# All first folds on VectorE, output additions in 128 pieces of 2 KB, a planner that counts transfers, and new ranks

## The chip, the cores and the metric

The kernel runs on one core of one Trainium2 chip. The metric is the device time of one execution in microseconds (us). In the texts, TensorE (PE in the profile) does matrix multiplications, VectorE (DVE) and ScalarE (ACT) work on elements, GpSimd (POOL) only issues DMA transfers here, and SyncE (SP) issues the other DMA transfers. What can be told from no change in a measurement of this kernel is about 0.5%, which is 1.9 us.

## What is computed

The output is a gated sum of two branches over the same x of 2048 x 512 numbers (float32). Branch a is a two-dimensional Fourier transform, a product with a filter, and the transform back. Branch b is a two-layer network with 1792 hidden columns.

```python
def _A_ref(x, w_r, w_i):
    B, S, D = x.shape
    X = jnp.fft.rfft2(x, axes=(-2, -1))
    X = X * (w_r + 1j * w_i)
    return jnp.fft.irfft2(X, s=(S, D), axes=(-2, -1))

def _B_ref(x, w1, b1, w2, b2):
    h = _gelu(jnp.einsum("bsd,df->bsf", x, w1) + b1)
    return jnp.einsum("bsf,fd->bsd", h, w2) + b2

x = A_x
g = _sigmoid((x * gate_w).sum(-1, keepdims=True))
return g * _A_ref(x, A_w_r, A_w_i) + (1 - g) * _B_ref(x, B_w1, B_b1, B_w2, B_b2)
```

## The kernel before

**Planning.** The program first builds a graph of 1877 steps: `v` for VectorE, `a` for ScalarE, `m` for a group of matmuls, `dma` for a transfer from SyncE, and `dma_pool` and `acc` for transfers from GpSimd. An `acc` adds to what stands at its destination. Each step carries an estimated cost, and a rank from the tuple `RANKS`, one entry for each step in the order in which the graph is built. The entry divided by 100 is the rank. `Graph.schedule` then plays the steps through: an engine that is free takes the ready step of the lowest rank for which buffer slots are free. The order that comes out is the order in which the instructions are written to each engine's queue, and on the chip each queue runs in that order. The ranks have the size of microseconds, but they fix an order and nothing else.

**Forward transform** (`forward(j)`, lines 670 to 767). It is done for 16 row tiles j, in the order `NORD` = 0, 4, 8, 12, 1, 5, 9, 13, 2, 6, 10, 14, 3, 7, 11, 15. Each tile of x (128 x 4 x 128) is folded twice: sums and differences of its halves give `eo`, and sums and differences of the halves of `eo` give `cl`. The second fold is always done on VectorE (line 698). The first fold has two forms. For the first `FOLD_DMA` = 12 tiles it is two VectorE instructions of 128 x 256 (line 684). For the last four, j = 3, 7, 11, 15, x is loaded into `eo`, ScalarE negates half of it (line 678), and GpSimd loads x again in the other order and adds it there. The result is split into a high and a low part (`eoh`, `eol`), and TensorE multiplies them with a table (`pd`), then with another (`py`); the sums are left in `Y[j]`.

**Middle.** `stage1`, `filt` and `stage4` are the short transform over the 16 tiles and the filter, all on VectorE. Beside them TensorE works on the network: `mlp(half, c)` takes half of the hidden columns for a quarter c of the rows. Groups `ph` are the first layer, twelve matmuls each, `po` the second. The result of the first half goes to DRAM (`bacc`); that of the second half is added there by `acc`, except for c = 2.

**Back transform and output.** `inverse(c, h)` runs for four c and two h. It scales the tile (`sw`, `pq`), splits it (`vh`, `vl`), multiplies (`pz`), splits again (`zh`, `zl`) and multiplies (`pa`). ScalarE copies half of `pa` to `od` (line 995), two VectorE instructions give `uv` (line 998), and the two output parts are the sum and the difference of the two halves of `uv`. For c = 3 and 0 (`ADD_DMA`) these are formed in DRAM: SyncE stores one half of `uv` to both parts, ScalarE makes the negative of the other half, and GpSimd adds it and its negative. For c = 1 (`SUM_FIRST`) VectorE forms both (`y`, line 1009) and GpSimd adds them to the output, where SyncE has already stored the network's share. For c = 2 VectorE forms both, GpSimd adds the network's first half to them (`y<-bb`), and `last` takes the second half off (`o`, line 1137). `combine(c, h)` reads `bacc` back into `ba` through GpSimd (line 513), multiplies it with 1 − g on VectorE (line 1028) and adds or stores it to the output.

**Queues.** All GpSimd transfers are issued strictly one behind the other, and so are SyncE's. A part of the output, `part(c, h, k)`, is 128 x 2 x 256 numbers, 2 KB in a row for each of 128 rows. In `uv` before, the halves are stored as `uv[:, i]`, and the transfer takes `uv[:, :, 0]` or `uv[:, :, 1]`: two runs of 1 KB that do not touch, so 256 pieces for a transfer of 256 KB. The same holds for `y`, which has rows of 257 numbers of which 256 are taken.

Of the kernel before, what the change touches and what calls it, by code (L numbers as in the profile page):

```python
# [117 lines left out]
FOLD_DMA = 12  # L118
# [51 lines left out]
class Graph:  # L170
# [283 lines left out]
def tile_kernel(ctx: ExitStack, tc: tile.TileContext, xt, w1, w2, b1, b2, x0g, wf, wrev, out, consts):  # L454
# [40 lines left out]
    def v(emit, n, reads, writes, rank=BULK, more=0.0):  # L495
        return add("vec", c_vec(n) + more, 0.12, emit, reads, writes, rank)
# [8 lines left out]
    def dma(emit, kb, reads, writes, rank=FEED, first=None):  # L505
        if first is not None:
            return add("sp", kb / 390, first, emit, reads, writes, rank)
# [747 lines left out]
```

## Time and profile before

| what | value |
|---|---|
| median of 3 runs | 389.84 us (389.78 to 391.7) |
| the profiled execution, its own time | 392.12 us |
| its span, first to last instruction | 390.4 us |
| TensorE busy | 370.8 us, 95% |
| VectorE busy | 325.9 us, 84% |
| ScalarE busy | 229.7 us, 59% |
| GpSimd busy | 64.5 us, 17% |
| granted TensorE clock, mean | 0.975 |
| DMA packets, MB | 53044, 64.30 |

The durations come from the one profiled execution, whose own time is 2.3 us above the median. [...] Where several matmuls follow without a wait, TensorE counts as busy also when the clock granted to it is low, so the clock has to be read beside the busy time. Idle time of an engine on which nothing waits costs nothing.

### The profile page before, as it was taken

The numbers are of one execution on the slowest core, as the hardware profiler recorded it, in microseconds if no ns is written. First come the engines' busy times: TensorE is split into PE (matmuls) and PEld (weight loads), VectorE is DVE, ScalarE is ACT, GpSimd is POOL, SyncE is SP. The second block draws the span as 40 slices with busy tenths as digits, with TensorE's granted clock in tenths as the row PEclk, the third lists the DMA queues.
The fourth block names the chain that finished last, engine by engine and source line by source line (L and its number), as shares of the span: only waits on it lengthen the run. The fifth ranks groups of instructions, "written<-read, shape, count | busy, mean of one in ns | idle before, by whom it ended". The sixth has DMA issues, their size and how long they took to land.

```text
span 390.4 us, 5587 instructions
## 1 busy us (share of the span) xinstructions
PE 370.8 (95%) x1838; PEld 313.5 (80%) x1838; DVE 325.9 (84%) x687; ACT 229.7 (59%) x457; POOL 64.5 (17%) x74
## 2 busy tenths in 40 slices
PE   8999999998999999999999999999978999999980
PEld 6888888886888888888888888888857888788870
DVE  4999998887899699999979998767737767999950
ACT  5865758886757542663665129946925496369400
POOL 0000000220000000121211120023342223423131
PEclk9999999998999999999999999999996999999995
DMA  8955996467772233696795751287688887855276
GB/s 270 372 158 155 311 346 220 97 149 177 222 220 89 61 107 110 111 266 164 138 266 140 225 82 41 71 250 137 98 145 168 186 241 98 133 121 148 82 126 90
DMA packets 53044, 64.30 MB, mean 165 GB/s; under 512 B 4784, under 2 KB 35824, under 8 KB 52240
## 3 DMA queue, kind: packets, MB, share of 16 engines
q1 hardware_dynamic: 41512, 46.39, 36.9%
q0 software_dynamic: 11360, 17.31, 29.0%
q10 hardware_dynamic: 144, 0.26, 0.3%
q8 instruction: 14, 0.23, 0.2%
q14 instruction: 14, 0.11, 0.1%
HBM read 39.69 MB, written 23.21 MB: 161 GB/s over the span
## 4 chain that ended last, share of the span: by engine, by line
PE 70%; DMA 8%; issue 8%; DVE 7%; POOL 3%; ACT 3%; POOLq 0%; SPq 0%; DVEq 0%; ACTq 0%
PE ph L526 31%; PE po L526 30%; PE pz L526 3%; PE pd L526 2%; PE py L526 2%; POOL out L517 2%; DMA eo<-in_xt 2%; DMA ba<-bacc 2%; PE pa L526 2%; DMA out<-uv 1%; DVE uv L998 1%; DMA xr<-in_xt 1%; DMA tf<-tf 1%; ACT ph L1086 1%; DVE y L763 0%
## 5 line engine op out<-in xcount | busy, mean ns | idle before, releaser
L1086 ACT ACTIVATE ph<-ph,b1t 128x512 f32<-128x512 f32 x56 | 36.8, 657 | 47.2 <-PE ph L526 47.0
L945 ACT ACTIVATE sw<-y,al 64x512 f32<-64x512 f32 x32 | 22.9, 721 | 3.6 <-DVE y L808 2.7
L904 DVE TENSOR_TENSOR m<-y,wf 128x514 f32<-128x514 f32 x32 | 20.7, 689 | 0.1
L1122 ACT ACTIVATE o<-po,b2t 128x512 f32<-128x512 f32 x16 | 11.0, 687 | 15.8 <-PE po L526 15.7
L517 POOL DMA_DIRECT2D eo<-in_xt x4 | 5.0, 1256 | 82.1 <-DMA tf<-tf 67.6
L517 POOL DMA_DIRECT2D bacc<-o x12 | 11.2, 983 | 38.7 <-ACT o L1125 35.8
L952 DVE SCALAR_TENSOR_TENSOR pq<-y,al,sw 128x256 f32<-128x256 f32 x32 | 14.5, 480 | 3.4 <-ACT sw L948 3.3
L1125 ACT ACTIVATE o<-po 128x512 f32<-128x512 f32 x12 | 7.0, 594 | 17.1 <-PE po L526 10.2
L1028 DVE SCALAR_TENSOR_TENSOR ba<-gb,ba 128x512 f32<-128x512 f32 x12 | 8.2, 686 | 7.9 <-DMA ba<-bacc 7.9
L526 PE MATMUL pd<-cf,eoh 128*128 128x260 f32 x64 | 13.0, 286 | 1.7 <-DVE x3l L735 1.7
L998 DVE TENSOR_TENSOR uv<-pa,od 128x512 f32<-128x512 f32 x16 | 10.5, 686 | 4.6 <-ACT od L995 4.6
L513 POOL DMA_DIRECT2D ba<-bacc x12 | 10.0, 835 | 24.7 <-DMA bacc<-o 10.0
L517 POOL DMA_DIRECT2D out<-y x8 | 9.0, 1128 | 27.9 <-DVE y L1009 11.0
L526 PEld LDWEIGHTS pd<-cf,eoh 128*128 128x128 f32 x64 | 10.7, 189 | 3.1 <-issue 1.9
L517 POOL DMA_DIRECT2D wa7l<-in_w x1 | 0.9, 924 | 67.4 <-PE po L526 67.4
L760 ACT ACTIVATE y<-pys 64x257 f32<-64x257 f32 x24 | 10.0, 418 | 3.2 <-DVE pys L757 2.8
L995 ACT ACTIVATE od<-pa 128x512 f32<-128x512 f32 x8 | 4.8, 597 | 10.6 <-PE pa L526 10.4
L526 PE MATMUL pd<-cf,eol 128*128 128x130 f32 x64 | 10.5, 254 | 0.0
L948 ACT ACTIVATE sw<-y 1x512 f32<-1x512 f32 x16 | 9.9, 627 | 0.4
L526 PEld LDWEIGHTS pd<-cf,eol 128*128 128x128 f32 x64 | 9.8, 189 | 0.4 <-DVE eol L701 0.2
L517 POOL DMA_DIRECT2D out<-ba x8 | 7.7, 1000 | 12.1 <-DVE ba L1028 7.2
L517 POOL DMA_DIRECT2D y<-bb x8 | 7.6, 954 | 11.0 <-DVE y L1009 6.2
(711 smaller groups left out, 1390.5 us busy)
## 6 DMA issues: line engine op xcount, KB each, us to landing
wf<-in_wf SPq DMA_DIRECT2D x16, 257.0 KB, 3.5
bacc<-o SPq DMA_DIRECT2D x16, 256.0 KB, 4.3
war<-in_w SPq DMA_DIRECT2D x14, 256.0 KB, 2.9
wbr<-in_w SPq DMA_DIRECT2D x14, 256.0 KB, 2.8
xm<-in_xt SPq DMA_DIRECT2D x12, 256.0 KB, 4.5
bacc<-o POOLq DMA_DIRECT2D x12, 256.0 KB, 4.8
ba<-bacc POOLq DMA_DIRECT2D x12, 256.0 KB, 3.5
xr<-in_xt SPq DMA_DIRECT2D x11, 256.0 KB, 4.2
```

Of the source, the lines that this page charges most:

```text
L513: return add("pool", kb / 300, 3.2, lambda: nc.gpsimd.dma_start(dst(), src()), reads, writes, rank)
L517: return add("pool", kb / 150, 3.4, lambda: nc.gpsimd.dma_start(dst(), src(), accum_op=ALU.add), reads, writes, rank)
L526: pe.matmul(ps, w, x, start=start, stop=stop)
L760: a(lambda o=o, i=i: act.activation(Y[j].ap()[o:o + HP, 1], pys.ap()[i:i + HP, 1], AF.Copy), 257, [(pys, 1)], [(Y[j], 1 + k)], 0, more=0.1)
L904: v(lambda mk=mk, k=k, y=y, w=w: vec.tensor_tensor(mk.ap(), y.ap(), w.ap()[:, k:k + 1, :ND].to_broadcast([P, 2, ND]), op=ALU.mult), 514, [ ...
L945: a(lambda sw=sw, y=y, o=o, i=i: act.activation(sw.ap()[o:o + HP], y.ap()[i:i + HP, ::-1, :HD], AF.Copy, scale=al.ap()[i:i + HP, 0:1]), 51 ...
L948: a(lambda sw=sw, y=y, j=j: act.activation(sw.ap()[HP:HP + 1], y.ap()[HP:HP + 1, ::-1, :HD], AF.Copy, scale=math.cos(math.pi * j / NJ)), 5 ...
L952: v(lambda sw=sw, pq_=pq_, y=y, j=j, k=k, op=op: vec.scalar_tensor_tensor(pq_.ap()[:, k], y.ap()[:, k, :HD], al.ap()[:, 1 + j:2 + j], sw.a ...
L998: v(lambda i=i, op=op: vec.tensor_tensor(uv.ap()[:, i], ps.ap()[:, 0], od.ap(), op=op), 512, [ps, od], [(uv, i)], 2)
L1028: vec.scalar_tensor_tensor(b.ap(), gg, 1.0, b.ap(), op0=ALU.subtract, op1=ALU.mult)
L1086: a(lambda f=f, ps=ps: act.activation(ps.ap(), ps.ap(), AF.Gelu_apprx_tanh, bias=b1t.ap()[:, f:f + 1]), 600, [b1t], [ps], 0.9 if half else ...
L1122: a(lambda o=o, ps=ps, q=q: act.activation(o.ap(), ps.ap(), AF.Identity, scale=-1.0, bias=b2t.ap()[:, q:q + 1]), 600, [b2t, ps], [o])
```

## The change

It has four parts.

First, `FOLD_DMA` goes from 12 to 16, the number of tiles. The branch with the negation and the accumulating load is then never taken, and the tiles 3, 7, 11 and 15 are folded like the others: one load and two VectorE instructions. The number of steps stays at 1877.

Second, `uv` is written so that each half of the later sum is contiguous (`uv[:, :, i]` is written, `uv[:, 0]` and `uv[:, 1]` are read), and the sums and negatives are written to a contiguous stretch of their tile (`flat`), except for c = 2. Every transfer from `uv` or from such a stretch then has 128 pieces of 2 KB.

Third, each transfer step takes a token in the planner: `ring` with three slots for GpSimd's, `hw` with eight for SyncE's. A token holds its slot from the start of the step to its estimated end, so no more than so many transfers are out at once in the plan. The tokens become no instruction and no memory. The sizes of two pools and of the scratch memory get names and keep their values.

Fourth, all 1877 ranks are new.

```diff
-FOLD_DMA = 12
+FOLD_DMA = 16
+RING, TI, TTAB = 3, 3, 3
+SCRATCH = 1024
...
 RANKS = (
...
 )
...
-    slots = {..., "ttab": 3, ..., "pm": 4, "ti": 3}
+    slots = {..., "ttab": TTAB, ..., "pm": 4, "ti": TI, "ring": RING, "hw": 8}
...
     def dma(emit, kb, reads, writes, rank=FEED, first=None):
+        reads = [*reads, buf("hw", [1], cls=len(g.steps))]
...
     def dma_pool(dst, src, kb, reads, writes, rank=FEED):
+        reads = [*reads, buf("ring", [1], cls=len(g.steps))]
...
     def acc(dst, src, kb, reads, writes, rank=FEED):
+        reads = [*reads, buf("ring", [1], cls=len(g.steps))]
...
-            v(lambda i=i, op=op: vec.tensor_tensor(uv.ap()[:, i], ps.ap()[:, 0], od.ap(), op=op), 512, [ps, od], [(uv, i)], 2)
+            v(lambda i=i, op=op: vec.tensor_tensor(uv.ap()[:, :, i], ps.ap()[:, 0], od.ap(), op=op), 512, [ps, od], [(uv, i)], 2)
+
+        def flat(y):
+            return y.ap().rearrange("p a b -> p (a b)")[:, :4 * P].rearrange("p (a b) -> p a b", a=2)
+
         if c in ADD_DMA:
             n = Y[c + 8 * h]
-            a(lambda: act.activation(n.ap()[:, :, :2 * P], uv.ap()[:, :, 1], AF.Copy, scale=-1.0), 512, [uv], [n], 2)
+            a(lambda: act.activation(flat(n), uv.ap()[:, 1], AF.Copy, scale=-1.0), 512, [uv], [n], 2)
             for k in range(2):
-                dma(lambda k=k: sp.dma_start(part(c, h, k), uv.ap()[:, :, 0]), 256, [uv], [(OUT[c], 2 * h + k)], 4)
-            acc(lambda: part(c, h, 0), lambda: uv.ap()[:, :, 1], 256, [uv], [(OUT[c], 2 * h)], 4)
-            acc(lambda: part(c, h, 1), lambda: n.ap()[:, :, :2 * P], 256, [n], [(OUT[c], 2 * h + 1)], 4)
+                dma(lambda k=k: sp.dma_start(part(c, h, k), uv.ap()[:, 0]), 256, [uv], [(OUT[c], 2 * h + k)], 4)
+            acc(lambda: part(c, h, 0), lambda: uv.ap()[:, 1], 256, [uv], [(OUT[c], 2 * h)], 4)
+            acc(lambda: part(c, h, 1), lambda: flat(n), 256, [n], [(OUT[c], 2 * h + 1)], 4)
             return
...
-            v(lambda w=w, op=op: vec.tensor_tensor(w.ap()[:, :, :2 * P], uv.ap()[:, :, 0], uv.ap()[:, :, 1], op=op), 512, [uv], [w])
+            v(lambda w=w, op=op: vec.tensor_tensor(w.ap()[:, :, :2 * P] if c == 2 else flat(w), uv.ap()[:, 0], uv.ap()[:, 1], op=op), 512, [uv], [w])
             if c in SUM_FIRST:
-                acc(lambda k=k: part(c, h, k), lambda w=w: w.ap()[:, :, :2 * P], 256, [w], [(OUT[c], 2 * h + k)], 4)
+                acc(lambda k=k: part(c, h, k), lambda w=w: flat(w), 256, [w], [(OUT[c], 2 * h + k)], 4)
...
-    nc = bacc.Bacc("TRN2", ..., dynamic_dma_scratch_size=1024)
+    nc = bacc.Bacc("TRN2", ..., dynamic_dma_scratch_size=SCRATCH)
```

Some ranks of steps that the next section names, before and after: the addition of `uv30` to the output 266.11 and 259.21, that of `ba030` to the same place 262.02 and 265.58; the last group of `pa11` 359.59 and 362.46; the first and the last of the final 14 matmul groups 371.75 and 376.56 before, 363.31 and 368.08 after; the last two additions of y, 369.51 and 370.46 before, 368.13 and 369.66 after.

More of the change, by code (lines that the diff above doesn't have):

```diff
@@ L465, in tile_kernel @@
     vec, act, pe, sp = nc.vector, nc.scalar, nc.tensor, nc.sync
-    slots = {"xr": 3, "xm": 4, "wra": 3, "wrb": 2, "t2k": 7, "e2": 4, "z": 4, "ttab": 3, "xhl": 2, "wa": 2 * FA, "wb": 2 * FA, "hid": 2 * FA,
-             "so": 2, "ba": 2,  "pf": 2, "pm": 4, "ti": 3}
+    slots = {"xr": 3, "xm": 4, "wra": 3, "wrb": 2, "t2k": 7, "e2": 4, "z": 4, "ttab": TTAB, "xhl": 2, "wa": 2 * FA, "wb": 2 * FA, "hid": 2 * FA,
+             "so": 2, "ba": 2,  "pf": 2, "pm": 4, "ti": TI, "ring": RING, "hw": 8}
     whole = ("xr", "xm", "wra", "wrb", "e2", "z", "ttab", "xhl", "wa", "wb", "hid", "so", "ba", "ctab", "gb")
@@ L1008, in inverse @@
             w = Y[c + 8 * h + 4 * k]
-            v(lambda w=w, op=op: vec.tensor_tensor(w.ap()[:, :, :2 * P], uv.ap()[:, :, 0], uv.ap()[:, :, 1], op=op), 512, [uv], [w])
+            v(lambda w=w, op=op: vec.tensor_tensor(w.ap()[:, :, :2 * P] if c == 2 else flat(w), uv.ap()[:, 0], uv.ap()[:, 1], op=op), 512, [uv], [w])
             if c in SUM_FIRST:
-                acc(lambda k=k: part(c, h, k), lambda w=w: w.ap()[:, :, :2 * P], 256, [w], [(OUT[c], 2 * h + k)], 4)
+                acc(lambda k=k: part(c, h, k), lambda w=w: flat(w), 256, [w], [(OUT[c], 2 * h + k)], 4)
             elif c != 2:
-                dma(lambda w=w, k=k: sp.dma_start(part(c, h, k), w.ap()[:, :, :2 * P]), 256, [w], [(OUT[c], 2 * h + k)], 4)
+                dma(lambda w=w, k=k: sp.dma_start(part(c, h, k), flat(w)), 256, [w], [(OUT[c], 2 * h + k)], 4)
     def part(c, h, k):
@@ L1235 @@
     wf = wf[rows][:, :, :, FORD]
-    nc = bacc.Bacc("TRN2", target_bir_lowering=False, num_devices=1, dynamic_dma_scratch_size=1024)
+    nc = bacc.Bacc("TRN2", target_bir_lowering=False, num_devices=1, dynamic_dma_scratch_size=SCRATCH)
     arrays, args = {}, []
```

220 rows, old and new, of the table RANKS are left out of this document.

## Prediction

> **What bounds the kernel now.** First I read the granted clock by slices on the page, then a table of stretches around its dips. Its columns: stretch and length; busy us of TensorE, its weight loads, VectorE, ScalarE and GpSimd, each with its instructions; granted clock; DMA share and GB/s.
>
> ```profile
> PEclk9999999998999999999999999999996999999995
> ...
> 90.90:92.70 1.80, 0.06 (x2) 0.05 (x1) 1.80 (x5) 0.47 (x2) 0.00 (x0) 1.00 0.35 109
> 94.65:98.06 3.41, 3.41 (x11) 2.73 (x11) 3.41 (x10) 2.46 (x7) 0.00 (x0) 0.50 0.89 258
> 289.80:294.30 4.50, 0.09 (x2) 0.07 (x1) 4.15 (x9) 3.02 (x7) 1.73 (x2) 0.81 1.07 156
> 294.30:299.45 5.15, 5.15 (x16) 4.45 (x17) 3.39 (x7) 2.31 (x5) 1.87 (x2) 0.50 0.81 215
> 379.15:390.40 11.25, 0.00 (x1) 0.00 (x0) 0.84 (x2) 0.00 (x0) 2.84 (x3) 0.60 0.57 82
> 0.00:379.15 379.15, 370.77 (x1838) 313.52 (x1838) 325.11 (x685) 229.71 (x457) 61.67 (x72) 0.99 0.67 167
> 334.00:373.20 39.20, 39.20 (x203) 33.41 (x202) 38.06 (x71) 22.53 (x38) 11.18 (x13) 1.00 0.54 119
> 264.00:334.00 70.00, 65.06 (x323) 55.06 (x323) 48.87 (x96) 43.38 (x76) 23.77 (x26) 0.95 0.80 153
> ```
>
> TensorE sets the time for almost all of the span: up to its last matmul at 379.15 it is idle for only 379.15 − 370.77 = 8.4 us. So the change can win in three places alone. One is a **tail** of 11.25 us in which TensorE does nothing. The second is a **stall** near 290: TensorE works 0.09 us of 4.50, and the 5.15 us after it run at clock 0.50. The third is a smaller stall near 91, 0.06 of 1.80 us, again with 3.41 us at clock 0.50 soon after. VectorE is the next engine: 97% busy (38.06 of 39.20) late, but only 48.87 of 70.00 between 264 and 334.
>
> Then the timeline of the tail: GpSimd's issues, and what feeds them.
>
> ```profile
> 369.57 1.08 POOL L517 DMA_DIRECT2D out<-y  x1 [10.97 <-DVE y L1009]
> ...
> 374.22 1.12 POOL L517 DMA_DIRECT2D out<-y  x1 [3.56 <-DVE o L1137]
> ...
> 374.81 1.46 POOL L517 DMA_DIRECT2D y<-bb  x1
> ...
> 376.11 1.29 DVE L1009 TENSOR_TENSOR y<-uv 128x512 f32<-128x512 f32 x2
> ...
> 378.88 0.86 POOL L517 DMA_DIRECT2D y<-bb  x1 [2.61 <-issue]
> 379.29 0.42 DVE L1137 TENSOR_TENSOR o<-y,po 128x256 f32<-128x256 f32 x1 [1.89 <-PE po L526]
> 379.56 1.33 POOL L517 DMA_DIRECT2D out<-y  x1
> 381.63 0.42 DVE L1137 TENSOR_TENSOR o<-y,po 128x256 f32<-128x256 f32 x1 [1.92 <-DMA y<-bb]
> 384.34 1.10 POOL L517 DMA_DIRECT2D out<-y  x1 [3.45 <-issue]
> ```
>
> ```profile
> out<-y POOLq DMA_DIRECT2D x8, 256.0 KB, 4.3
> out<-ba POOLq DMA_DIRECT2D x8, 256.0 KB, 5.1
> ```
>
> The last two sums y were both ready at 376.11 + 1.29 = 377.40, yet they were issued at 379.56 and 384.34. The distances 369.57 to 374.22 (4.65), 374.22 to 378.88 (4.66) and 379.56 to 384.34 (4.78) are each the 4.3 us landing of an out<-y plus a little: one such transfer (256 pieces of 1 KB) and one y<-bb (128 pieces) go out together, and the next waits for the landing. "Issue" is the profile's word for a wait that it cannot name. Compare a stretch of two reads into ba and two y<-bb, all four gone within 3.2 us (the first and the last):
>
> ```profile
> 354.55 0.75 POOL L513 DMA_DIRECT2D ba<-bacc  x1 [3.11 <-DVE pq L952]
> ...
> 357.73 0.87 POOL L517 DMA_DIRECT2D y<-bb  x1 [0.31 <-issue]
> ```
>
> Last, the chain of waits into the stall near 290 (start, length, what).
>
> ```profile
> 276.38 1.06 POOL out L517
> 277.44 3.52 issue
> 280.97 1.09 POOL out L517
> 282.06 0.76 POOL ba L513
> 282.82 2.97 issue
> 285.79 3.17 DMA ba<-bacc
> ...
> 292.27 0.52 ACT od L995
> ...
> 292.82 1.30 DVE uv L998 x2
> ...
> 294.26 1.94 PE pz L526 x8
> 296.20 7.14 PE ph L526 x24
> ```
>
> It is the same cause as in the tail. A 1 KB accumulation (280.97) blocks the next read into ba until 285.79; VectorE waits for that read (6.00 us, in the row below); behind it on VectorE stands pq, behind pq on ScalarE v12h and od, behind od the two uv, and only they free the PSUM tile that TensorE's next pz needs. The two PE pieces at the end also price the slow clock.
>
> **The change part by part.** *Pieces of 2 KB.* uv is laid out so that each output row pair is contiguous, so the 12 additions from uv, its negative and y have 128 pieces, not 256 (SP's eight out<-uv stores too). The arithmetic stays. If 128-piece transfers overlap as above, the tail loses its ring waits: with TensorE's end unchanged, y is ready at 377.40, the second issue is at about 377.7 (0.9 after the first), it lands 5.1 us later (the out<-ba row, the dearer of the two; 4.3 by the other), at 382.8. Before, the last issue at 384.34 landed by 388.6 and the span ended 1.8 later; so the end moves to 384.6. **Tail: 390.4 − 384.6 = 5.8 us.** The last o is no obstacle: it waited at 381.63 for y<-bb, which no longer stands behind an out<-y, and can run after the one at 379.29; its store lands before 384. Below, the gain is 0 if the limit counts transfers and not pieces; above, it is 6.6 (landing 4.3).
>
> [...]
>
> *The stall near 290.* Without the blocking, the ba read issued at 285.79 goes right behind the one at 282.06, about 3 us sooner, and the out and ba steps before it (276.38, 280.97) lose their 3.52 too; 6.5 us of cover against a stall of 4.5. So it should go whole. Its price is the idle time in the table of waits (total, times, longest), plus the half clock, from the same chain further up:
>
> ```profile
> 244.15 0.87 PE pz L526 x8
> 245.02 5.51 PE ph L526 x24
> ```
>
> ```profile
> DVE ba L1028 <- DMA ba<-bacc: 7.9, 2, 6.0
> PE pz L526 <- DVE uv L998: 4.9, 2, 4.4
> ```
>
> The same 8 pz and 24 ph take 6.38 there and 9.08 here: 2.7 us. With the second, 0.5 us wait of that row (4.9 in two): **4.9 + 2.7 = 7.6 us**. Below: 0, if the wait moves to ScalarE or another read.
>
> *All folds on VectorE.* For j = 3, 7, 11, 15 a load, a ScalarE negation and an accumulating GpSimd load give way to a load and two VectorE folds. The pieces that they replace and the price of a fold:
>
> ```profile
> 86.30 4.52 DMA eo<-in_xt
> ...
> 90.84 0.76 DVE cl L698 x2
> ...
> L684 DVE TENSOR_TENSOR eo<-xr 128x256 f32<-128x256 f32 x22 | 8.9, 418 | 0.0
> ```
>
> Eight more instructions: 8 × 0.418 = 3.3 us by mean length, 8 × 0.38 = 3.0 us as the pair of equal shape in 0.76 shows; I take 3.0. The 4.52 us landing ahead of the folds is gone, so the stall of 1.80 − 0.06 = 1.7 us should go, and half of the 3.41 us at clock 0.50, 1.7 us. **3.4 us**, bounds 0 and 3.4, and the 3.0 us of VectorE is paid below. The load in its place comes early, in SP's order, as its twelve siblings do; were it late, TensorE would wait as it did here.
>
> [...]
>
> *Ranks and the count of transfers in flight* change the order alone. In the new list the final 14 groups (po1_230, po1_23256) still follow pa11, and GpSimd's last four steps are unchanged (y14 and y6, then out1.2 and out1.3); earlier, out3.0 and out3.1 from uv30 now stand ahead of their ba030 and ba130 siblings (259.2 against 265.6 in the list). No row shows the new order, so I bound it. It cannot gain past the 8.4 us of idle time and 4.4 of half clock already counted. What it can lose is VectorE's time. To let TensorE end 7.6 + 3.4 = 11.0 us sooner, VectorE must be done 11.0 us sooner with 3.0 us more work, and from 334 on it has 1.1 us free. 7.9 us come from its waits for ba; 11.0 + 3.0 − 7.9 = 6.1 must come out of the other 13 us that it idles between 264 and 334. I put half, 3.0, on the path, and one new small stall like that near 91, with its half clock 1.7: **debit 4.7**, between 0 and 11.0 (both stalls come back elsewhere).
>
> **Sum:** 5.8 + 7.6 + 3.4 − 4.7 = 12.1 us off. The durations come from an execution of 392.12 us with span 390.4; the median of the runs is 389.84, 2.3 below. Taken off the median: 389.84 − 12.1 = **377.7**.
>
> **Rivals.** *Only the tail is won* (debit 11.0): VectorE, 97% busy late, is the bound behind TensorE. For it: 38.06 of 39.20. Against it: 21 us idle just before. 389.84 − 5.8 = 384.0. *No effect:* the limit on GpSimd's queue counts transfers, or SP's order spoils what it gives; the folds' 3.4 are eaten by their 3.0: 389.4. Against it: the three equal distances above, after 1 KB transfers alone. *Slower, by a queue that blocks in order:* GpSimd issues strictly one behind the other, and a wait for a sum stops every read behind it, as the 10.97 us at 369.57 shows where nothing was needed behind it. If the new order puts such a sum ahead of a ba read that VectorE needs, TensorE stalls 11.0 and pays the 2.7 of half clock: + 13.7; the stall near 290 stays, and only tail and folds come off: 389.84 + 13.7 − 9.2 = 394.3. It decides as soon as such a blocking exceeds the tail's and the folds' 9.2 us beyond its cover. For it: out3.0 and out3.1 from uv moved ahead. Against it: there the sums are what was last ready anyhow.
>
> **How the numbers follow.** Forecast 0.66, only the tail 0.22, no effect 0.04, slower 0.08. Below lies the sum with no debit, 389.84 − 16.8 = 373.0; above, the tail-only case with a tail 2.5 us less good. I take 373.5 to 386.5, which leaves the two last rivals and the far low end outside. A change within 0.5% (1.9 us) cannot be told from none here: faster 0.88, same 0.04, slower 0.08.
>
> **What would show it.** Right: no wait of 3 us before GpSimd's out issues; three 128-piece transfers in flight; the two last out<-y within 1.5 us of each other; TensorE's end to span's end under 7 us; clock 0.50 nowhere between 90 and 360; VectorE's fold row at x30 or a like count, no eo on GpSimd. Wrong: "issue" distances of 4.6 us after 2 KB transfers (the pieces do not count); TensorE's waits moved to VectorE's rows in 330 to 370 (the debit was too small); or long waits of GpSimd for VectorE with ba reads behind them (the third rival).

## The result and the profile after

| | before | after |
|---|---|---|
| median, same chip | 389.81 us | 374.67 us (373.85 to 375.61) |
| ratio | | 0.9604, 95% interval 0.9565 to 0.9644 |
| profiled execution, its own time | 392.12 us | 374.5 us |
| its span | 390.4 us | 372.7 us |
| TensorE busy until its last matmul | 370.77 of 379.15 us | 365.98 of 367.03 us |
| from there to the end | 11.25 us | 5.67 us |
| DMA packets, MB | 53044, 64.30 | 49395, 63.25 |

The change takes 15.1 us off the median; 12.1 were forecast. Ratios here and below, but not medians, leave out the three executions that took over 1.5% longer than the fastest of their kernel (395.09, 395.21 and, at a mean clock of 0.752, 460.76 us). The profile after has the answers to the rows of before. First the granted clock of the page, then the table of stretches (columns as in the prediction), then all the waits of TensorE that the table of waits knows.

```profile
PEclk9999999999999999999999999999999999999999
```

```profile
0.00:367.03 367.03, 365.98 (x1838) 310.47 (x1838) 326.65 (x693) 227.47 (x453) 56.69 (x70) 1.00 0.66 170
367.03:372.70 5.67, 0.00 (x1) 0.00 (x0) 0.75 (x2) 0.00 (x0) 0.00 (x0) 0.96 0.68 126
264.00:334.00 70.00, 70.00 (x363) 59.75 (x362) 55.16 (x110) 46.88 (x83) 23.71 (x29) 1.00 0.82 169
334.00:367.00 33.00, 33.00 (x190) 28.40 (x188) 31.07 (x58) 17.76 (x29) 11.96 (x14) 1.00 0.59 130
```

```profile
PE none L530 <- DVE zero L593: 1.1, 1, 1.1
```

Once TensorE has started, it does not stop, and no slice has a low clock. The one wait left is that for its first operand. Between 264 and 334 VectorE now does 55.16 us of work and not 48.87. So the difference of the spans, 17.7 us, parts without remainder: idle TensorE up to its last matmul 8.38 − 1.05 = 7.3; shorter busy time 370.77 − 365.98 = 4.8, nearly all of it the half clock; tail 11.25 − 5.67 = 5.6. (The spans differ by more than the medians because the profiled execution of before lay 2.3 us above its median.)

The issues of GpSimd and the last work of VectorE in the tail, from the timeline:

```profile
357.38 1.77 POOL L521 DMA_DIRECT2D out<-y  x2 [6.07 <-DVE y L1018]
362.28 1.75 POOL L521 DMA_DIRECT2D y<-bb  x2 [3.14 <-DVE bb L1112]
365.04 1.76 POOL L521 DMA_DIRECT2D out<-y  x2 [1.00 <-DVE y L1018]
```

```profile
363.99 1.29 DVE L1018 TENSOR_TENSOR y<-uv 128x512 f32<-128x512 f32 x2
367.07 0.75 DVE L1146 TENSOR_TENSOR o<-y,po 128x256 f32<-128x256 f32 x2 [1.79 <-PE po L530]
```

Each pair of out<-y that stood 4.65 and 4.78 us apart is now one entry of two, both issued within 1.8 us, and each waits for VectorE's y and for no unnamed thing. The last pair is out at 365.04 + 1.76 = 366.80, before TensorE's end. A single transfer did not become quicker:

```profile
out<-y POOLq DMA_DIRECT2D x8, 256.0 KB, 5.2
out<-ba POOLq DMA_DIRECT2D x8, 256.0 KB, 5.5
```

The medians are 5.2 us to landing against 4.3 before, and 5.5 against 5.1: side by side each takes longer, and together they are done sooner (the last pair of out<-y 6.17 us after its first issue, 365.04 to 371.21; before, 9.17, 379.56 to 388.73).

Of the signs that the prediction named, one did not come as written. GpSimd's out issues still have waits of 3 us and more ahead of them, such as the 6.07 us above, but those have a named releaser, and TensorE waits for none of them. One read into ba still waits 3.7 us for nothing that the profile names.

### The profile page after: what moved, and what is told of

Its sections match the earlier page's. It is cut to its first block, busy times and chain, and to the rows that moved or that the text cites. A ratio compares the mean times of both kernels' runs of the same rounds, so it can differ in the third digit from the quotient of the medians.

```text
span 372.7 us, 5574 instructions
## 1 busy us (share of the span) xinstructions
PE 366.0 (98%) x1838; PEld 310.5 (83%) x1838; DVE 327.4 (88%) x695; ACT 227.5 (61%) x453; POOL 56.7 (15%) x70
## 2 busy tenths in 40 slices
DMA packets 49395, 63.25 MB, mean 170 GB/s; under 512 B 4720, under 2 KB 29616, under 8 KB 48592
## 4 chain that ended last, share of the span: by engine, by line
PE 98%; DVE 0%; DVEq 0%; issue 0%
PE po L530 42%; PE ph L530 41%; PE pz L530 4%; PE pd L530 4%; PE py L530 3%; PE pa L530 3%; PE none L530 1%; DVE o L1146 0%; DVEq L1256 0%; PE pown L530 0%; DVE zero L593 0%
## 5 line engine op out<-in xcount | busy, mean ns | idle before, releaser
L688 DVE TENSOR_TENSOR eo<-xr 128x256 f32<-128x256 f32 x30 | 11.9, 417 | 0.0
L999 ACT ACTIVATE od<-pa 128x512 f32<-128x512 f32 x8 | 4.8, 596 | 11.2 <-PE pa L530 11.0
L702 DVE TENSOR_TENSOR xr<-eo 128x256 f32<-128x256 f32 x24 | 9.7, 417 | 0.1
L704 ACT ACTIVATE eoh<-xr 128x512 fp32r<-128x512 f32 x12 | 7.6, 634 | 2.4 <-PE pd L530 2.3
L521 POOL DMA_DIRECT2D out<-y x8 | 7.8, 1000 | 7.6 <-DVE y L1018 7.1
```

The lines of the kernel that those rows point to most:

```text
L521: return add("pool", kb / 150, 3.4, lambda: nc.gpsimd.dma_start(dst(), src(), accum_op=ALU.add), reads, writes, rank)
L688: v(lambda s=s, op=op: vec.tensor_tensor(eo.ap()[:, s], x.ap()[:, 0:2], x.ap()[:, 2:4], op=op), 256, [x], [(eo, s)], FEED)
L702: v(lambda k=k, op=op: vec.tensor_tensor(quarter(cl, k), eo.ap()[:, :, 0], eo.ap()[:, :, 1], op=op), 256, [eo], [(cl, k)] if j % 4 == 0 or ...
```

## The experiments

Twelve kernels, in three groups; the kernels of a group ran beside the kernel before on one chip. The chips differ a little (393.08, 391.95 and 392.65 us for the kernel before), so ratios are compared, and a gain in us is (1 − ratio) times that group's time of before.

| kernel | median, us | ratio to before, 95% interval | gain, us |
|---|---|---|---|
| before, 2 KB pieces alone | 377.84 | 0.9616 (0.9565 to 0.9667) | 15.1 |
| before, folds alone | 390.99 | 0.9929 (0.9894 to 0.9964) | 2.8 |
| before, pieces and folds | 377.04 | 0.9596 (0.9546 to 0.9646) | 15.9 |
| before, scratch of 1472 bytes | 376.78 | 0.9581 (0.9534 to 0.9627) | 16.5 |
| after, 1 KB pieces | 384.54 | 0.9808 (0.9729 to 0.9887) | 7.5 |
| after, four folds by DMA | 383.12 | 0.9773 (0.9699 to 0.9847) | 8.9 |
| before, new ranks and tokens alone | 391.97 | 0.9982 (0.9935 to 1.003) | 0.7 |
| after, planned without tokens | 375.04 | 0.9568 (0.9508 to 0.9629) | 16.9 |
| before, pieces for c = 1 alone | 386.9 | 0.9871 (0.9817 to 0.9925) | 5.1 |
| before, pieces for c = 3 and 0 alone | 383.01 | 0.9758 (0.9714 to 0.9802) | 9.5 |
| after, scratch of 1472 bytes | 375.06 | 0.9550 (0.9512 to 0.9587) | 17.7 |
| after, scratch of 640 bytes | 376.84 | 0.9596 (0.9554 to 0.9637) | 15.9 |

### The 2 KB pieces alone

The output part of `inverse` is taken from the changed kernel; ranks, folds and plan are those of before.

```diff
-            v(lambda i=i, op=op: vec.tensor_tensor(uv.ap()[:, i], ps.ap()[:, 0], od.ap(), op=op), 512, [ps, od], [(uv, i)], 2)
+            v(lambda i=i, op=op: vec.tensor_tensor(uv.ap()[:, :, i], ps.ap()[:, 0], od.ap(), op=op), 512, [ps, od], [(uv, i)], 2)
...
```

> Before, with the 2 KB pieces alone: the old order, the old folds. Theory (pieces make room in GpSimd's queue, and both the tail and the stall near 290 were waits for room): tail 5.8 us and stall 7.6 us come off, 389.8 - 13.4 = 376.4 us, with 374 to 380 for what VectorE may give back; no gap over 1 us in TensorE near 290, last two out<-y issued within 1.5 us. Rival (the new order is what removes the stall): only the tail, 384.0 us, with the 4.4 us gap near 290 still there. Second rival (queue counts transfers): 389.8 us.

The gain is 15.1 us; the ratio is the full change's within the intervals (0.9616 and 0.9604). From its waits of TensorE and its GpSimd timeline:

```profile
PE pd L526 <- DVE x3l L735: 2.0, 1, 2.0
```

```profile
360.51 0.86 POOL L517 DMA_DIRECT2D out<-y  x1 [10.85 <-DVE y L1014]
361.71 0.87 POOL L517 DMA_DIRECT2D out<-y  x1 [0.34 <-DVE y L1014]
362.26 1.22 POOL L517 DMA_DIRECT2D y<-bb  x1
364.80 0.89 POOL L517 DMA_DIRECT2D y<-bb  x1 [1.32 <-issue]
368.12 1.77 POOL L517 DMA_DIRECT2D out<-y  x2 [2.43 <-DVE y L1014]
```

The wait of pz for uv, 4.9 us before, is not in the list any more; the small stall near 91 is. The last two out<-y go together. The theory of room in the queue holds. The rival, that only the new order can remove the stall, falls; the order of the instructions here is that of before.

### The same room in another way

Before, with one number changed, so that the pieces stay at 1 KB.

```diff
-    nc = bacc.Bacc(..., dynamic_dma_scratch_size=1024)
+    nc = bacc.Bacc(..., dynamic_dma_scratch_size=1472)
```

> Before, unchanged but for the scratch memory of the GpSimd transfers, 1472 bytes instead of 1024. Theory (waits for room in that memory): two 1 KB transfers now fit at once, so the waits of 4.6 us between them go, as with the 2 KB pieces: about 376.4 us, 374 to 381. Rival (what limits is the landing of the transfer before, or a count of transfers): no change, 389.8 us, with the distances of 4.65 us still there.

16.5 us, within the intervals the same as the pieces give. Its GpSimd timeline:

```profile
360.22 1.44 POOL L517 DMA_DIRECT2D y<-bb  x1
363.11 0.86 POOL L517 DMA_DIRECT2D y<-bb  x1 [1.45 <-issue]
366.10 2.21 POOL L517 DMA_DIRECT2D out<-y  x2 [2.12 <-DVE y L1009]
```

Two additions of 256 pieces are now issued one behind the other, in 2.21 us. So what bound the kernel was the room that this scratch memory gives to GpSimd's transfers, and neither the length of a piece nor the order. This shows it without touching the data layout.

This kernel also loses the small stall near 91, though its four folds by DMA are still there. Its waits of TensorE, but for the one for the first operand (the 0.5 us lie near 53):

```profile
PE ph L526 <- ACT mxh L645: 0.6, 1, 0.6
PE pd L526 <- DVE x5l L735: 0.5, 1, 0.5
```

The accumulating loads into eo, in the kernel before and then here:

```profile
81.52 1.21 POOL L517 DMA_DIRECT2D eo<-in_xt  x1 [3.83 <-DVE x14l L734]
86.30 1.23 POOL L517 DMA_DIRECT2D eo<-in_xt  x1 [3.57 <-DVE y L754]
```

```profile
81.72 2.47 POOL L517 DMA_DIRECT2D eo<-in_xt  x2 [3.91 <-DVE x14l L734]
```

Such a load reads x in two runs of 1 KB for each row, so it has 256 pieces too. Before, the load at 81.52 landed at 85.98, and the last one was issued 0.32 us later; with more room the two go together. So the stall near 91 was a third wait for room, which the prediction did not see. The releaser that the profile names for the load at 86.30, VectorE's y, is a coincidence: in this kernel the same y ends at 86.54, and the load has been out since 82.63.

### The tail and the stall apart

The new layout for one value of c only; `new` chooses between the two layouts.

```diff
+        new = c == 1          # the other kernel: c in ADD_DMA
...
-            v(... uv.ap()[:, i] ...)
+            v(... (uv.ap()[:, :, i] if new else uv.ap()[:, i]) ...)
```

> Before, with 2 KB pieces for c = 1 alone, so in the four additions of y at the end; c = 3 and 0 keep 1 KB. Theory (tail and stall near 290 are two separate waits for room): only the tail's 5.8 us come off, ratio 0.985, with the 4.4 us gap near 290 still there. Rival (one wait feeds the other): more than 9 us off, or none.

> Before, with 2 KB pieces for c = 3 and 0 alone, so in the eight additions before 330; the last four of y keep 1 KB. Theory: the stall near 290 and its half clock go, 7.6 us, ratio 0.980, and the tail keeps its 11 us. Rival: the time won at 290 is lost again in the tail, which the queue ends, ratio 0.99 or more.

The waits of TensorE in the first (c = 1):

```profile
PE pz L526 <- DVE uv L999: 6.4, 2, 4.6
PE pd L526 <- DVE x3l L735: 1.5, 1, 1.5
```

and in the second (c = 3 and 0), with its GpSimd timeline:

```profile
PE pd L526 <- DVE x3l L735: 1.6, 1, 1.6
```

```profile
360.08 1.08 POOL L517 DMA_DIRECT2D out<-y  x1 [10.98 <-DVE y L1020]
364.67 1.12 POOL L517 DMA_DIRECT2D out<-y  x1 [3.50 <-DVE o L1148]
365.25 1.46 POOL L517 DMA_DIRECT2D y<-bb  x1
369.19 0.86 POOL L517 DMA_DIRECT2D y<-bb  x1 [2.48 <-issue]
369.93 1.26 POOL L517 DMA_DIRECT2D out<-y  x1
374.72 1.10 POOL L517 DMA_DIRECT2D out<-y  x1 [3.53 <-issue]
```

The tails of the two, from TensorE's last matmul to the end of the span:

```profile
377.69:384.10 6.41, 0.00 (x1) 0.00 (x0) 0.42 (x1) 0.00 (x0) 0.00 (x0) 0.81 0.63 115
369.66:380.40 10.74, 0.01 (x1) 0.00 (x0) 0.84 (x2) 0.00 (x0) 2.63 (x3) 0.65 0.54 86
```

The first keeps the stall near 290 (4.6 us), shortens the tail from 11.25 to 6.41 us, and wins 5.1 us (2.9 to 7.2). The second has no stall near 290, keeps a tail of 10.74 us with distances of 4.6 and 4.8 us, and wins 9.5 us (7.8 to 11.2). So these are two separate waits with one cause. That 5.1 + 9.5 = 14.6 comes so near to the 15.1 for both is partly chance: in the first the waits of pz for uv grow from 4.9 to 6.4 us, and neither kernel has the half clock near 95, so that its 1.7 us is in both gains.

### Folds alone, and pieces with folds

```diff
-FOLD_DMA = 12
+FOLD_DMA = 16
```

> Before, with all first folds on VectorE alone: old ranks, 1 KB pieces. Theory: the 1.7 us stall near 91 and 1.7 us of half clock go, 389.8 - 3.4 = 386.4 us; the stall near 290 and the tail stay. Rival (VectorE's 3.0 us of more work comes out on TensorE's path): 389.4 us or more, with new TensorE gaps between 56 and 130.

> Before, with the 2 KB pieces and the folds, old ranks and no count of transfers. Theory (the two edits carry the gain and add up): 389.8 - 13.4 - 3.4 = 373.0 us, as fast as the changed kernel's 374.7 or a little faster. Rival (the new order is needed, since VectorE is the next bound): 377.7 us or more, with new TensorE gaps after 300.

The folds alone give 2.8 us (1.4 to 4.2). The waits of TensorE that matter here, and two stretches:

```profile
PE pz L526 <- DVE uv L998: 6.7, 2, 5.5
PE py L526 <- ACT x7h L733: 0.4, 1, 0.4
PE pd L526 <- DVE x11l L735: 0.3, 1, 0.3
```

```profile
287.30:292.75 5.45, 0.00 (x1) 0.03 (x1) 4.92 (x10) 2.97 (x7) 1.73 (x2) 0.96 1.04 145
292.75:299.18 6.43, 6.42 (x19) 5.46 (x20) 4.20 (x9) 2.35 (x5) 2.62 (x3) 0.50 0.73 180
```

The stall near 91 shrinks to 0.4 and 0.3 us, but what TensorE wins there it mostly stands again later: the waits of pz for uv grow from 4.9 to 6.7 us (and VectorE's for ba from 7.9 to 9.7), and TensorE works 6.43 us at half clock after it, not 5.15. The slow stretch itself is as long as before, 6.83 and 6.82 us; the work only starts earlier in it. With the pieces, the folds bring 15.9 against 15.1 us, which the intervals do not tell apart. The rival that needed the new order falls: with the old ranks, pieces and folds reach the full change's ratio (0.9596 and 0.9604).

### What the new order does

> Before, with the new ranks and the count of transfers alone: 1 KB pieces, four folds by DMA. Theory (the order carries little by itself): 389.8 minus at most 2 us, 387.8 us or more, tail still near 11 us. Rival (the order carries most of the 15.1 us): 380 us or less.

> The changed kernel with its new ranks, planned without the count of transfers that may be out. Theory (the tokens only fit the plan to what the queue does, and the pieces make room anyway): within 2 us of 374.7. Rival (the ranks are tuned to the plan with tokens, so the order loses its spacing and TensorE gets new gaps with half clock after them): 378 us or more.

> The changed kernel with the old layout of uv and y, so 1 KB pieces again; new order, new folds. Theory (room in the queue): the tail's 5.8 us come back, 374.7 + 5.8 = 380.5 us, and with the waits in the middle of the queue up to 7.6 more, 388; out issues 4.6 us apart. Rival (the new order itself, with its count of transfers, spaces them so that pieces no longer matter): 374.7 to 376 us.

> The changed kernel with the last four first folds by DMA again. Theory: the stall near 91 with its half clock returns, 374.7 + 3.4 = 378.1 us. Rival (TensorE had other work to do there in the new order): 374.7 us, since VectorE then has 3.0 us less to do.

The edits are those of the diff, undone one at a time: the layout and `FOLD_DMA = 12` together for the first, the three lines that add tokens for the second, the layout for the third, `FOLD_DMA = 12` for the fourth.

New ranks and tokens alone win nothing that can be told (0.7 us, from −1.2 to 2.5). That is a trade and not an absence of effect. TensorE has no wait between 260 and 340 in this kernel, but it waits 3.8 us near 93, where it waited 1.7 before, with the clock at 0.50 from 98.01 to 104.84, and 2.2 us near 347; the tail is 11.8 us.

```profile
PE py L530 <- DVE g_6l L577: 3.8, 1, 3.8
PE ph L530 <- DVE g_10l L577: 2.2, 1, 2.2
```

Without the tokens the changed kernel is as fast as with them (ratios 0.9568 and 0.9604, within each other's intervals). That says little of tokens in general, since the plan without them writes nearly the same order: in the traces 12 of TensorE's 1838 instructions and 2 of GpSimd's 70 stand at another place. The changed kernel itself did not run in this group, so that kernel without tokens, 375.04 us, stands for it. Against it, 1 KB pieces cost 384.54 − 375.04 = 9.5 us in the new order; 11.04 us of tail are back, and two waits of 2.2 and 1.6 us in TensorE:

```profile
PE pa L530 <- DVE z20l L979: 2.2, 1, 2.2
PE ph L530 <- DVE g_10l L577: 1.6, 1, 1.6
```

```profile
371.46:382.50 11.04, 0.00 (x0) 0.00 (x0) 0.84 (x2) 0.00 (x0) 3.09 (x3) 0.74 0.56 84
```

In the new order the stall near 290 is not there even with 1 KB pieces; the two waits stand near 321 and 340, and no half clock follows them. So the order alone can remove that stall as well, but not the tail. The folds by DMA cost 383.12 − 375.04 = 8.1 us in the new order, more than twice the 3.4 expected. The stretches show the stall and the half clock soon after it:

```profile
93.80:97.70 3.90, 0.00 (x0) 0.00 (x0) 2.61 (x6) 0.66 (x4) 0.00 (x0) 1.00 1.12 347
98.13:101.54 3.41, 3.07 (x10) 2.19 (x9) 3.37 (x9) 1.91 (x4) 0.00 (x0) 0.50 1.11 368
```

VectorE waits there for the last accumulating load, and g_6l, which TensorE needs, stands behind that fold in its queue:

```profile
95.09 0.76 DVE L702 TENSOR_TENSOR cl<-eo 128x256 f32<-128x256 f32 x2 [3.43 <-DMA eo<-in_xt]
```

The last three of the four loads were each issued 0.3 us after the landing of the one before (78.22, 83.49 and 89.18), so this is the wait for room near 91 again. Why it costs more in the new order was not tested.

### More room and less

```diff
-SCRATCH = 1024
+SCRATCH = 1472     # the other kernel: 640
```

> [...] TensorE has no gap left, so only the tail can gain: 0 to 1 us, 374 to 375 us. Rival (three at a time still hold GpSimd back where it counts): 372 us or less.

> The changed kernel with scratch memory of 640 bytes: by the theory two transfers of 128 pieces fit, not three, as one of 256 and one of 128 did before. If room is what was bought, GpSimd waits again at its out issues: 2 to 8 us slower than the changed kernel, 377 to 383 us, with TensorE gaps between 260 and 340. Rival (one piece layout is simply quicker to land): no change, 374.7 us.

More room wins nothing (375.06 us), as expected where TensorE has no gap. With less, GpSimd's issues are spaced by unnamed waits again:

```profile
268.74 0.88 POOL L521 DMA_DIRECT2D out<-ba  x1 [2.31 <-issue]
270.17 0.87 POOL L521 DMA_DIRECT2D out<-uv  x1 [0.55 <-issue]
273.08 0.75 POOL L517 DMA_DIRECT2D ba<-bacc  x1 [2.05 <-issue]
275.11 0.76 POOL L517 DMA_DIRECT2D ba<-bacc  x1 [1.28 <-issue]
```

Each of the four starts 0.3 us after the landing of the transfer two places before it. But the loss is 376.84 − 375.06 = 1.8 us against the other kernel of this pair, below the 2 to 8 expected; the executions of the two kernels do not overlap (374.31 to 375.66 and 375.88 to 377.75), though the intervals of their ratios do. TensorE has one gap of 0.6 us. Two transfers at a time are nearly enough in the new order with the new pieces. That the greater loss with 1 KB pieces comes from this, that two additions of 256 pieces can't be out together at all, is inferred and was not tested by itself.

## Why the prediction was right, point by point

**The bound.** TensorE's two stalls and the tail were the three places to win, and all three were won; 365.98 of 367.03 us are busy now. All three had one cause, which the prediction saw for two of them.

**The tail,** predicted 5.8 us: 5.6 between the spans; in the kernel that changes c = 1 alone the tail is 11.25 − 6.41 = 4.8 us shorter. The span ends 5.67 us after TensorE's last matmul; worked out were 384.6 − 379.15 = 5.45.

**The stall near 290,** predicted 7.6 us: 9.5 (7.8 to 11.2) by the kernel that changes c = 3 and 0 alone. The mechanism, a ba read behind a 1 KB addition, is shown by the pieces alone and, with the pieces as they were, by the larger scratch. About 1.7 us of the difference is the half clock near 95, which I had put to the folds: it is missing in that kernel too, whose stall near 91 is still there. What the sum did not have is that the new order by itself removes this stall as well.

**The folds,** predicted 3.4 us: 2.8 alone (1.4 to 4.2). Here the size is partly right by chance. The stall near 91 goes, but the sum put it down to the 4.52 us landing of the last load by DMA, and what made that load late was a wait for room: more scratch removes the stall with the folds left as they were. The half clock was no fixed part of it: the kernels with the pieces keep a stall of 1.5 to 2.0 us at that place, and no half clock follows.

```profile
91.00:93.00 2.00, 0.02 (x2) 0.03 (x1) 1.84 (x5) 0.44 (x2) 0.00 (x0) 1.00 0.38 118
93.00:103.00 10.00, 9.88 (x58) 8.48 (x59) 9.91 (x26) 7.39 (x23) 0.00 (x0) 1.00 0.81 234
```

These two stretches are of the kernel with the pieces alone; before, after a stall of 1.7 us, the clock was 0.50 from 94.65 to 98.06. So the length of a stall does not say whether a slow stretch follows: a stall of 2.0 us had none behind it where one of 1.7 had 3.41 us. What decides it, no run here shows. Whether 3.4 us or 1.7, the stall without its half clock, is nearer, the measured interval of 1.4 to 4.2 does not decide.

**The debit for VectorE,** predicted 4.7 us between 0 and 11.0: this is the term that was mis-sized, and in the traces it measured 0. I had put half of 6.1 us, which VectorE was to find between 264 and 334 beyond its waits for ba, on the path, and a new small stall beside it. In that stretch VectorE does 55.16 − 48.87 = 6.3 us more, which is less than the 7.9 us of waits for ba that are gone; another 240.42 − 234.84 = 5.6 us more is done before 264. The path saw none of it. With the pieces alone, in the old order, it does 56.83 us in that stretch, 8.0 more, without a wait for ba, and TensorE has no gap over 0.2 us after 100. The step that failed is that I took an engine that is 97% busy late for one without reserve: its work could be done in the time in which it had waited for the same queue. With the debit at 0 the forecast would have been 373.0 by its own sum, below the range's low end of 373.5 and 1.7 us below the measured 374.67: the terms were read from an execution 2.3 us above the median and taken off the median. The debit turned a forecast 1.7 us too low into one 3.0 us too high.

**The rivals.** "Only the tail" (384.0), with VectorE as the bound, fell: with the larger pieces TensorE has no wait for VectorE late in the kernel. The kernel with c = 1 alone comes near its time (0.9871 of 389.84 is 384.8), but because the stall near 290 is still there. "No effect" falls by every kernel with more room. "Slower, by a queue that blocks in order" did not come: with the new ranks out<-uv (267.67) stands ahead of the ba reads (270.25 and 271.52), and TensorE does not wait. The ranks and tokens alone are within what can be told from no change, as the forecast, which gave them no gain of their own, had it. How the ranks would do with still other piece lengths was not tried.

## What to carry to other kernels

When a queue's transfers start at fixed distances of about one landing time (here 4.65 and 4.66 us, with a median landing of 4.3), and the profile names no releaser, or one that another run shows not to matter, look for a limit on what may be out, and count it in pieces and not in transfers: making the runs contiguous (15.1 us here) or giving the queue more scratch memory (16.5 us) freed both the tail and a stall far from it. Price a stall of TensorE with the slow clock that may follow, but as a chance and not as a fixed part (here 3.41 us at 0.50 after a stall of 1.7 us, none after one of 2.0). An engine that is nearly full late may owe that to its own waiting earlier, on the same cause (VectorE here: 97% busy late, after 7.9 us of waits for ba): look at what it does in the stretch before, and charge nothing for it twice.

## What the runs showed of the hardware

The room in the scratch memory goes by pieces: at 1024 bytes an addition in 256 pieces and a transfer in 128 were out together, and the next waited for the landing and was issued 4.66 us after the addition; in 128 pieces three were out. In the tail of the kernel before, each next issue follows such a landing by 0.3 us (landed 373.91, 378.56 and 384.02; issued 374.22, 378.88 and 384.34). Counted from the issue and landing times of all GpSimd transfers (a read into ba, 128 rows of 2 KB, as 128 pieces), there were at 1024 bytes never more out at once than three of 128 pieces, or one of 256 and one of 128 (the kernels before, after, and with the pieces alone); at 1472 bytes two of 256 and one of 128, or four of 128; at 640 bytes two of 128. 448 bytes more were worth 16.5 us, as much as the new layout. How many bytes one piece takes, no run shows.

The landing of one addition was not shortened by longer pieces, though the wait was (median 4.3 us in 256 pieces, 5.2 in 128, where more of them overlap).
